# Chunk attention and token MLP: PSUM as two separate two-bank tiles used in turn, one evacuation per two output tiles and two transposed blocks, a new order of units

## The chip, the cores and the metric

The kernel runs on one core of one Trainium2 chip. Times are device microseconds (us) of one execution; each is the median of the runs named. Of 11 runs of the kernel before (176.16 to 180.61 us), 9 lie within a per cent of their median, 177.84 us. Runs more than 1.5% above the fastest of the same kernel in a call are set apart as slow, and ratios use the fast runs alone. A ratio is the mean time of one kernel's fast runs over that of the other's fast runs of the same rounds, so it is not quite the ratio of the medians that are quoted. The span of a profile is about 2 us shorter than the time of the same run. Experiments ran on three different chips, so versions of different calls are compared through their ratio to the kernel before of the same call.

Engines: PE is TensorE, DVE is VectorE, ACT is ScalarE, POOL is GpSimd.

## The reference, cut to what matters

```python
# q, k, v: (8, 8, 576, 64); chunks of 64 tokens attend only to themselves
scores = scale * q_c @ k_c.T;  attn = softmax(scores);  x = attn @ v_c      # x: (8, 576, 512)
# token MLP on x of each batch
wq = x @ w_q;  wk = x @ w_k                       # 512 -> 64
mixed = (wq @ wk.T * scale) @ x                   # (wq @ (wk.T @ x)) is cheaper
out = relu(mixed) @ w_out                         # 512 -> 512, float32
```

## The kernel before

One batch after the other goes through the same units, and each unit is a burst of matmuls on PE into PSUM and one evacuation by ACT or DVE. S is scores and exp (four per batch), A is attention times V with normalisation (four), X transposes one 128-wide block of x (four), Q and K are the two projections, G is wk.T @ x, M is one of four mixes with Relu, and O is one output tile of 128 rows (4.5 per batch). In iteration b the attention of batch b is interleaved with the MLP of batch b-1. PSUM is divided into four two-bank tiles: `st` for scores, `xp` for attention, `mp` for X, Q, G and M, and `op` for K and O.

```python
    mp = ps.tile([P, 2, 512], F32, name="mp")
    op = ps.tile([P, 2, 512], F32, name="op")
...
    def xtr(b, i, bank):
        tx = mp[:, bank, :].bitcast(F16)
        for j in range(NJ):
            nc.tensor.transpose(
                tx[:, j * P : j * P + P], xn[b % 2][:, j, i * P : i * P + P], ident[:]
            )
        nc.vector.tensor_copy(xt[b % 2][i][:], tx[:, 0 : NJ * P])
...
    def mix(b, i, half):
        for h in range(2):
            nc.tensor.matmul(
                mp[:, h, 0:HS],
                lhsT=g16[b % 2][CH * h : CH * h + CH, i * P : i * P + P],
                rhs=wqT[b % 2][CH * h : CH * h + CH, half * HS : half * HS + HS],
                ...
            )
        nc.scalar.activation(rmx..., mp[:, :, 0:HS], AF.Relu, scale=scale_moe)
...
    def o_(cnt=1):
            ...
            for i in range(NI):
                nc.tensor.matmul(
                    op[:, n % 2, :],
                    lhsT=rmx[pr % 2][:, i, tl * P : tl * P + P],
                    rhs=wout[:, i, :],
                    ...
                )
            nc.scalar.copy(os_[:], op[:, n % 2, :])
            nc.sync.dma_start(of[n * P : n * P + P, :], os_[:])
...
    # per batch:  S0 A3' X2' O S1 A0 X3' O Q' K' S2 A1 G' O S3 A2 M' M' O M' M' X0 O X1   (' = batch b-1)
```

The softmax here doesn't subtract the row's maximum and nothing guards it: scores larger than these inputs give would overflow.

## Time and profile before

| | before |
|---|---|
| median of 3 runs | 177.56 us (176.45 to 180.11) |
| profiled span (a run of 179.53 us, not one of the three) | 177.6 us |
| PE / DVE / ACT busy | 117.6 / 74.3 / 70.0 us |
| mean granted PE clock | 0.866 |
| last packet of the loads | 102 us |

These are lines of the first two parts of the page of the kernel before: busy time of PE in us and share of the span, then, over 40 equal slices of the span (4.4 us each), the granted PE clock and the busy share of the DMA engines in tenths.

```profile
PE 117.6 (66%) x2400; PEld 71.8 (40%) x2400; DVE 74.3 (42%) x149; ACT 70.0 (39%) x117; POOL 49.5 (28%) x49
...
PEclk9999999996599569987998899789969996996555
DMA  2999999999999999999999931113103111320322
```

No compute engine is full: the busiest, PE, is at 66%. The DMA engines are at 9 tenths or more in every slice but the first until about 102 us. The clock dips in each batch and stays low at the end: the clock record of the trace has PE at 0.5 in seven stretches of 3.4 or 6.8 us between 41.4 and 150.7 us, and from 160.9 us to the end.

This is the chain of waits of the kernel before, in order of time (start us, us, engine, tile, line). The steps shown are the second kT transpose of four successive batches.

```profile
82.65 0.66 DVE kT L118
...
100.73 0.66 DVE kT L118
...
117.85 0.66 DVE kT L118
...
134.49 0.66 DVE kT L118
```

The pattern repeats every 17.3 us on average. So a batch takes about 17 us although PE is busy for only 13.7 us of it.

These are groups of instructions of the kernel before: line, engine, operation, tiles, shape and count, then busy us in total and mean ns of one, then the idle time of the engine just before them and what ended it.

```profile
L254 PE MATMUL op<-wout,rmx 128*128 128x512 f16 x144 | 47.5, 462 | 3.1 <-ACT osb L262 3.1
L181 PE MATMUL mp<-ident,xn 128*128 128x128 f16 x160 | 19.1, 268 | 9.8 <-ACT rmx L236 5.2 <-DVE xt L184 4.3
L184 DVE COPY xt<-mp 128x640 f16<-128x640 f16 x32 | 15.5, 485 | 34.6 <-PE mp L181 34.6
L228 PE MATMUL mp<-wqT,g 64*128 64x288 f16 x64 | 10.4, 307 | 18.1 <-ACT rmx L236 17.2 <-issue 0.9
```

The mixes (L228) hold PE idle for 18.1 us, nearly all of it waiting for the Relu that reads the same tile. The timeline of the kernel before shows one such stretch (start us, us, engine, line, operation; in brackets the idle time before and its releaser):

```profile
126.11 0.30 PE L228 MATMUL mp<-wqT,g 64*128 64x288 f16 x2
126.53 0.66 ACT L236 ACTIVATE rmx<-mp 128x576 f16<-128x576 f32 x1
127.24 0.30 PE L228 MATMUL mp<-wqT,g 64*128 64x288 f16 x2 [0.83 <-ACT rmx L236]
127.57 0.65 ACT L236 ACTIVATE rmx<-mp 128x576 f16<-128x576 f32 x1 [0.39 <-PE mp L228]
128.28 0.30 PE L228 MATMUL mp<-wqT,g 64*128 64x288 f16 x2 [0.74 <-ACT rmx L236]
...
130.35 0.69 PE L181 MATMUL mp<-ident,xn 128*128 128x128 f16 x5 [0.74 <-ACT rmx L236]
```

PE works 0.30 us and waits 0.74 us, again and again: PE, ACT and PE go through one tile in single file. The transposes that follow take 0.69 us for five, against 0.45 elsewhere in the steady part; the clock record has PE at half its clock from 130.2 to 133.6 us (granted clock 0.50 there, 1.00 from 126.0 to 130.2).

One more place in the same timeline matters, the output tiles at the end. They alternate between the two banks of one tile, yet each waits for the copy out of the other bank:

```profile
163.58 0.59 ACT L262 COPY osb<-op 128x512 f32<-128x512 f32 x1 [1.22 <-PE op L254]
164.21 1.86 PE L254 MATMUL op<-wout,rmx 128*128 128x512 f16 x4 [0.72 <-ACT osb L262]
...
166.79 1.86 PE L254 MATMUL op<-wout,rmx 128*128 128x512 f16 x4 [0.72 <-ACT osb L262]
```

The copy at 163.58 ends at 164.17 and the matmuls of the other bank start at 164.21. In this program a wait covers the whole PSUM tile, not the bank. Two banks of one tile are therefore no double buffer here.

### The profile page before, as it was taken

How to read it: one execution, taken by the hardware profiler on the slowest of the kernel's cores; microseconds unless marked ns; L12 is line 12 of the kernel's file. 1: busy time of each engine (PE TensorE's matmuls, PEld its weight loads, DVE VectorE, ACT ScalarE, POOL GpSimd, SP SyncE). 2: the span in 40 equal slices, each digit the busy share in tenths (PEclk: the TensorE clock that was granted, in tenths of full speed). 3: DMA queues.
4: the chain of work that ended last, by engine and by line, in shares of the span. 5: the costliest groups of instructions: out<-in, count | busy, mean ns of one | idle time of the engine just before them, and what ended most of it. 6: DMA issues, size and time to landing. Idle time of an engine off the chain costs nothing.

```text
span 177.6 us, 5290 instructions
## 1 busy us (share of the span) xinstructions
PE 117.6 (66%) x2400; PEld 71.8 (40%) x2400; DVE 74.3 (42%) x149; ACT 70.0 (39%) x117; POOL 49.5 (28%) x49
## 2 busy tenths in 40 slices
PE   0024350693998499759964988589578957955861
PEld 0023240471665257426632564257236624622220
DVE  2332634534565365536461656275619422410000
ACT  2021111055246435654473437454634572344121
POOL 7997736647263273372000000000000000000000
PEclk9999999996599569987998899789969996996555
DMA  2999999999999999999999931113103111320322
GB/s 25 173 165 184 176 167 182 162 182 167 176 207 224 209 175 197 243 201 196 224 222 196 151 125 63 59 63 122 59 0 122 60 65 59 118 99 19 118 98 79
DMA packets 81156, 24.56 MB, mean 138 GB/s; under 512 B 76016, under 2 KB 76528, under 8 KB 81136
## 3 DMA queue, kind: packets, MB, share of 16 engines
q0 software_dynamic: 75952, 14.81, 98.5%
q1 hardware_dynamic: 5184, 9.44, 14.6%
q8 instruction: 18, 0.29, 0.7%
q14 instruction: 2, 0.02, 0.0%
HBM read 29.62 MB, written 9.44 MB: 220 GB/s over the span
## 4 chain that ended last, share of the span: by engine, by line
PE 44%; DVE 17%; ACT 17%; DMA 14%; issue 4%; POOL 2%; ACTq 0%; POOLq 0%
PE op L254 19%; ACT rmx L236 10%; DMA kn<-in_k_dram 8%; DVE xn L169 7%; DMA vt<-in_v_dram 6%; PE mp L189 6%; PE mp L181 5%; ACT osb L262 5%; PE mp L228 4%; DVE xt L184 4%; PE xp L159 3%; PE mp L217 3%; PE op L203 3%; DVE kT L118 3%; DVE qT L118 2%
## 5 line engine op out<-in xcount | busy, mean ns | idle before, releaser
L254 PE MATMUL op<-wout,rmx 128*128 128x512 f16 x144 | 47.5, 462 | 3.1 <-ACT osb L262 3.1
L262 ACT COPY osb<-op 128x512 f32<-128x512 f32 x36 | 21.1, 586 | 48.1 <-PE op L254 42.5
L142 ACT ACTIVATE est<-st 128x640 f16<-128x640 f32 (+1 forms) x32 | 20.9, 652 | 29.1 <-PE st L134 28.9
L184 DVE COPY xt<-mp 128x640 f16<-128x640 f16 x32 | 15.5, 485 | 34.6 <-PE mp L181 34.6
L169 DVE TENSOR_TENSOR xn<-xp,rec 128x640 f16<-128x640 f32 x32 | 26.4, 824 | 1.1
L181 PE MATMUL mp<-ident,xn 128*128 128x128 f16 x160 | 19.1, 268 | 9.8 <-ACT rmx L236 5.2
L236 ACT ACTIVATE rmx<-mp 128x576 f16<-128x576 f32 x32 | 20.9, 653 | 10.0 <-PE mp L228 9.9
L134 PE MATMUL st<-qT,kT 32*64 32x64 f16 x1152 | 17.9, 209 | 9.5 <-DVE kT L118 8.6
L254 PEld LDWEIGHTS <-rmx 128*128 128x128 f16 x144 | 14.4, 112 | 20.6 <-issue 14.5
L228 PE MATMUL mp<-wqT,g 64*128 64x288 f16 x64 | 10.4, 307 | 18.1 <-ACT rmx L236 17.2
L67 POOL DMA_DIRECT2D qn<-in_q_dram x16 | 16.1, 1005 | 18.8 <-DMA vt<-in_v_dram 16.7
L159 PE MATMUL xp<-vt,est 64*64 64x65 f16 x576 | 12.8, 211 | 12.6 <-DVE xn L169 7.5
L134 PEld LDWEIGHTS <-kT 32*64 32x64 f16 x1152 | 14.0, 121 | 17.1 <-DVE kT L118 8.6
L181 PEld LDWEIGHTS <-xn 128*128 128x128 f16 x160 | 14.4, 120 | 16.0 <-issue 14.2
L67 POOL DMA_DIRECT2D kn<-in_k_dram x16 | 16.0, 1001 | 8.8 <-DMA qn<-in_q_dram 4.5
L118 DVE STREAM_TRANSPOSE qT<-qn 128x576 f32<-128x576 f32 x16 | 12.4, 772 | 9.3 <-DMA qn<-in_q_dram 9.3
L73 POOL DMA_DIRECT2D vt<-in_v_dram x8 | 14.7, 1834 | 4.3 <-DMA kn<-in_k_dram 4.0
L159 PEld LDWEIGHTS <-est 64*64 64x64 f16 x576 | 10.0, 119 | 14.0 <-issue 12.2
L118 DVE STREAM_TRANSPOSE kT<-kn 128x576 f32<-128x576 f32 x16 | 12.0, 748 | 3.3 <-DMA kn<-in_k_dram 3.3
L228 PEld LDWEIGHTS <-g 64*128 64x128 f16 x64 | 3.2, 94 | 24.7 <-issue 24.0
L168 DVE RECIPROCAL rec<-xp 128x10 f32<-128x10 f32 x32 | 6.8, 213 | 15.3 <-PE xp L159 15.0
L189 PE MATMUL mp<-xt,wqd 128*128 128x288 f16 x64 | 10.1, 305 | 2.4 <-DVE xt L184 1.3
(22 smaller groups left out, 46.9 us busy)
## 6 DMA issues: line engine op xcount, KB each, us to landing
out_dram<-osb SPq DMA_DIRECT2D x36, 256.0 KB, 2.1
qn<-in_q_dram POOLq DMA_DIRECT2D x16, 288.0 KB, 16.6
kn<-in_k_dram POOLq DMA_DIRECT2D x16, 288.0 KB, 16.9
vt<-in_v_dram POOLq DMA_DIRECT2D x8, 576.0 KB, 18.7
wout<-in_moe_w_out_dram POOLq DMA_DIRECT2D x1, 512.0 KB, 9.4
wqd<-in_moe_w_q_dram POOLq DMA_DIRECT2D x1, 64.0 KB, 8.0
wk<-in_moe_w_k_dram POOLq DMA_DIRECT2D x1, 64.0 KB, 7.6
```

The source lines that it names most:

```text
L67: nc.gpsimd.dma_start(dst[b][part][:], src[b].rearrange("(t p r) d -> p t (r d)", p=P, r=R)[:, a:e, :],)
L118: nc.vector.transpose(out=o.rearrange("p (t w r) -> p t r w", r=R, w=32), in_=src[b][part].bitcast(F32).rearrange("p t (r d) -> p t r d", ...
L134: nc.tensor.matmul(st[half : half + CH, i // 2, (t - a) * CH : (t - a) * CH + CH], lhsT=operand(kT, b, t, i, e), rhs=operand(qT, b, t, i, ...
L142: nc.scalar.activation(est[b % 2][s].rearrange("p i t c -> p i (t c)")[:, :, 0:n], st[:, :, 0:n], AF.Exp, scale=scale_attn,)
L159: nc.tensor.matmul(xp[CH * (c % 2) : CH * (c % 2) + CH, hh, jj * 66 : jj * 66 + 65], lhsT=est[b % 2][s][half : half + CH, i // 2, t - SETS ...
L169: nc.vector.tensor_tensor(out=xn[b % 2][:, :, 2 * kk * D : 2 * kk * D + 2 * D].rearrange("p j (i d) -> p i j d", i=2), in0=xpv[:, :, :, 0: ...
L181: nc.tensor.transpose(tx[:, j * P : j * P + P], xn[b % 2][:, j, i * P : i * P + P], ident[:])
L184: nc.vector.tensor_copy(xt[b % 2][i][:], tx[:, 0 : NJ * P])
L189: nc.tensor.matmul(mp[:, h, 0:HS], lhsT=wqd[:, i, :], rhs=xt[b % 2][i][:, h * HS : h * HS + HS], start=(i == 0), stop=(i == NI - 1),)
L236: nc.scalar.activation(rmx[(b // 2) % 2].rearrange("p (h i) n -> p i h n", h=2)[:, i, :, o : o + HS], mp[:, :, 0:HS], AF.Relu, scale=scale ...
L254: nc.tensor.matmul(op[:, n % 2, :], lhsT=rmx[pr % 2][:, i, tl * P : tl * P + P], rhs=wout[:, i, :], start=(i == 0), stop=(i == NI - 1),)
L262: nc.scalar.copy(os_[:], op[:, n % 2, :])
```

## The change

The intent is that the two PSUM tiles of the MLP become a true double buffer. Every unit outside S and A takes the other tile than the unit before it (`pair()`). X handles two blocks at once with one DVE copy of 1280 columns in place of two of 640, and O handles up to two output tiles with one ACT copy of 1024 columns and one DMA. The units come in a new order that spreads the O and the DVE work.

```diff
+ORDER = """
+S0 A3 O2 X1 S1 A0 Tq0 Q K S2 A1 G O2 X0 S3 A2 Tk0 M0 M1 Tq1 O1 M2 M3 Tk1
+"""
...
-    mp = ps.tile([P, 2, 512], F32, name="mp")
-    op = ps.tile([P, 2, 512], F32, name="op")
+    rp = [ps.tile([P, 2, 512], F32, name=f"rp{i}") for i in range(2)]
...
+    def pair():
+        ring["at"] += 1
+        return rp[ring["at"] % 2]
+
+    def xtr(b, n):
+        tx = pair().bitcast(F16)
+        for i in range(2):
+            for j in range(NJ):
+                nc.tensor.transpose(
+                    tx[:, i, j * P : j * P + P],
+                    xn[b % 2][:, j, (2 * n + i) * P : (2 * n + i) * P + P],
+                    ident[:],
+                )
+        nc.vector.tensor_copy(xt[b % 2][n][:], tx[:, :, 0 : NJ * P])
...
+    def mix(b, n):
+        i, half = n % 2, n // 2
+        a = pair()
...
+    def outp(most):
...
+        a = pair()
+        for u in range(m):
...
+        nc.scalar.copy(os_[:, 0:m, :], a[:, 0:m, :])
+        nc.sync.dma_start(
+            of[n * P : (n + m) * P, :].rearrange("(u p) m -> p u m", p=P),
+            os_[:, 0:m, :],
+        )
```

In the order, Tq and Tk are the stream transposes of q and k of the next batch on DVE; A3, X1, Q, K, G, M and O belong to batch b-1.

More of the change, by code (lines that the diff above doesn't have):

```diff
@@ L99 @@
     xn = [sb.tile([P, NJ, DM], F16, name=f"xn{i}") for i in range(2)]
-    xt = [[sb.tile([P, NJ * P], F16, name=f"xt{i}_{c}") for c in range(NI)] for i in range(2)]
+    xt = [[sb.tile([P, 2, NJ * P], F16, name=f"xt{i}_{c}") for c in range(2)] for i in range(2)]
     wqT = [sb.tile([P, S], F16, name=f"wqT{i}") for i in range(2)]
@@ L104 @@
     rmx = [sb.tile([P, NI, 2 * S], F16, name=f"rmx{i}") for i in range(2)]
-    NOSB = 6
-    osb = [sb.tile([P, DM], F32, name=f"osb{i}") for i in range(NOSB)]
+    NOSB = 4
+    osb = [sb.tile([P, 2, DM], F32, name=f"osb{i}") for i in range(NOSB)]
     for i in range(B):
@@ L112, with tr @@
         nc.vector.memset(xv[i][CH:P, NJ - 1, D : D + 2], 1.0)
-    def tr(b, part):
+    def tr(b, which):
+        part = int(which[1])
         a, e = TR[part]
-        for src, dst in ((qn, qT), (kn, kT)):
-            o = dst[b % 2].bitcast(F32)[:, CH * a : CH * e]
-            nc.vector.transpose(
-                out=o.rearrange("p (t w r) -> p t r w", r=R, w=32),
-                in_=src[b][part].bitcast(F32).rearrange("p t (r d) -> p t r d", d=32),
-            )
+        src, dst = (qn, qT) if which[0] == "q" else (kn, kT)
+        nc.vector.transpose(
+            out=dst[b % 2]
+            .bitcast(F32)[:, CH * a : CH * e]
+            .rearrange("p (t w r) -> p t r w", r=R, w=32),
+            in_=src[b][part].bitcast(F32).rearrange("p t (r d) -> p t r d", d=32),
+        )
     def operand(buf, b, t, i, e):
@@ L176, in attend, with mlp_q @@
         )
-    def xtr(b, i, bank):
-        tx = mp[:, bank, :].bitcast(F16)
-        for j in range(NJ):
-            nc.tensor.transpose(
-                tx[:, j * P : j * P + P], xn[b % 2][:, j, i * P : i * P + P], ident[:]
-            )
-        nc.vector.tensor_copy(xt[b % 2][i][:], tx[:, 0 : NJ * P])
-    def wq_(b):
+    ring = {"at": 0}
+    def pair():
[11 more added lines that the diff above has]
+        nc.vector.tensor_copy(xt[b % 2][n][:], tx[:, :, 0 : NJ * P])
+    def mlp_q(b):
+        a = pair()
         for i in range(NI):
@@ L189, in wq_ @@
                 nc.tensor.matmul(
-                    mp[:, h, 0:HS],
+                    a[:, h, 0:HS],
                     lhsT=wqd[:, i, :],
-                    rhs=xt[b % 2][i][:, h * HS : h * HS + HS],
+                    rhs=xt[b % 2][i // 2][:, i % 2, h * HS : h * HS + HS],
                     start=(i == 0),
@@ L196, in wq_, with mlp_k @@
         nc.scalar.copy(
-            wqT[b % 2].rearrange("p (h n) -> p h n", h=2), mp[:, :, 0:HS]
+            wqT[b % 2].rearrange("p (h n) -> p h n", h=2), a[:, :, 0:HS]
         )
-    def wk_(b, pool, bank):
+    def mlp_k(b):
+        a = pair()
         for j in range(NJ):
@@ L203, in wk_ @@
                 nc.tensor.matmul(
-                    pool[:, bank, j * DH : j * DH + DH],
-                    lhsT=xt[b % 2][i][:, j * P : j * P + P],
+                    a[:, 0, j * DH : j * DH + DH],
+                    lhsT=xt[b % 2][i // 2][:, i % 2, j * P : j * P + P],
                     rhs=wk[:, i, :],
@@ L210, in wk_, with mlp_g @@
         nc.vector.tensor_copy(
-            wkn[b % 2].rearrange("p j c -> p (j c)"), pool[:, bank, 0 : NJ * DH]
+            wkn[b % 2].rearrange("p j c -> p (j c)"), a[:, 0, 0 : NJ * DH]
         )
-    def gm_(b, bank):
+    def mlp_g(b):
+        a = pair()
         for j in range(NJ):
@@ L217, in gm_ @@
                 nc.tensor.matmul(
-                    mp[CH * h : CH * h + CH, bank, 0 : DM // 2],
+                    a[CH * h : CH * h + CH, 0, 0 : DM // 2],
                     lhsT=wkn[b % 2][:, j, :],
@@ L223, in gm_ @@
                 )
-        nc.scalar.copy(g16[b % 2][:], mp[:, bank, 0 : DM // 2])
-    def mix(b, i, half):
+        nc.scalar.copy(g16[b % 2][:], a[:, 0, 0 : DM // 2])
+    of = out.rearrange("b s m -> (b s) m")
+    done = {"out": 0, "ready": 0, "st": 0}
+    def mix(b, n):
+        i, half = n % 2, n // 2
+        a = pair()
         for h in range(2):
             nc.tensor.matmul(
-                mp[:, h, 0:HS],
+                a[:, h, 0:HS],
                 lhsT=g16[b % 2][CH * h : CH * h + CH, i * P : i * P + P],
@@ L237, in mix @@
             rmx[(b // 2) % 2].rearrange("p (h i) n -> p i h n", h=2)[:, i, :, o : o + HS],
-            mp[:, :, 0:HS],
+            a[:, :, 0:HS],
             AF.Relu,
@@ L241, in mix @@
         )
-    of = out.rearrange("b s m -> (b s) m")
-    state = {"n": 0, "ready": 0}
-    def o_(cnt=1):
-        for _ in range(cnt):
-            n = state["n"]
-            if n >= state["ready"]:
-                return
-            state["n"] = n + 1
-            pr, tl = n // NCH, n % NCH
+        if i == 1:
+            done["ready"] = ((2 * b + half + 1) * HS) // P
+    def outp(most):
+        n = done["out"]
+        m = min(most, done["ready"] - n, NCH - n % NCH)
+        if m <= 0:
+            return
+        done["out"] = n + m
+        a = pair()
+        for u in range(m):
+            pr, tl = (n + u) // NCH, (n + u) % NCH
             for i in range(NI):
                 nc.tensor.matmul(
-                    op[:, n % 2, :],
+                    a[:, u, :],
                     lhsT=rmx[pr % 2][:, i, tl * P : tl * P + P],
@@ L260, in o_ @@
                 )
-            os_ = osb[n % NOSB]
-            nc.scalar.copy(os_[:], op[:, n % 2, :])
-            nc.sync.dma_start(of[n * P : n * P + P, :], os_[:])
-    tr(0, 0)
-    tr(0, 1)
+        os_ = osb[done["st"] % NOSB]
+        done["st"] += 1
+        nc.scalar.copy(os_[:, 0:m, :], a[:, 0:m, :])
+        nc.sync.dma_start(
+            of[n * P : (n + m) * P, :].rearrange("(u p) m -> p u m", p=P),
+            os_[:, 0:m, :],
+        )
+    for w in ("q0", "k0", "q1", "k1"):
+        tr(0, w)
@@ L267 @@
     for b in range(B + 1):
         p = b - 1
-        if b < B:
-            scores(b, 0)
-        if p >= 0:
-            attend(p, 3)
-            xtr(p, 2, 0)
-        o_()
-        if b < B:
-            scores(b, 1)
-            attend(b, 0)
-        if p >= 0:
-            xtr(p, 3, 1)
-            o_()
-            if p == 0:
-                nc.vector.tensor_copy(wqd[:, :, DH : 2 * DH], wqd[:, :, 0:DH])
-            wq_(p)
-            wk_(p, op, state["n"] % 2)
-            state["n2"] = 1
@@ L286 @@
-        if b < B:
-            scores(b, 2)
-            attend(b, 1)
-        if p >= 0:
-            gm_(p, 0)
-            o_()
-        if b < B:
-            scores(b, 3)
-            attend(b, 2)
-        if b + 1 < B:
-            tr(b + 1, 0)
-        if p >= 0:
-            for half in range(2):
-                for i in range(2):
-                    mix(p, i, half)
-                    if i == 1 and half == 0:
-                        o_()
-            state["ready"] = (NCH * b) // 2
@@ L304 @@
-        if b < B:
-            xtr(b, 0, 0)
-            o_()
-            xtr(b, 1, 1)
-        if b + 1 < B:
-            tr(b + 1, 1)
-    o_(10)
+        for w in ORDER.split():
+            if w[0] == "T":
+                if b + 1 < B:
+                    tr(b + 1, w[1:])
+            elif w[0] == "O":
+                outp(int(w[1]))
+            elif w[0] == "S":
+                if b < B:
+                    scores(b, int(w[1]))
+            elif w[0] == "A":
+                kk = int(w[1])
+                bb = p if kk == 3 else b
+                if 0 <= bb < B:
+                    attend(bb, kk)
+            elif w[0] == "X":
+                i = int(w[1])
+                bb = p if i else b
+                if 0 <= bb < B:
+                    xtr(bb, i)
+            elif p >= 0:
+                if w == "Q":
+                    if p == 0:
+                        nc.vector.tensor_copy(wqd[:, :, DH : 2 * DH], wqd[:, :, 0:DH])
+                    mlp_q(p)
+                elif w == "K":
+                    mlp_k(p)
+                elif w == "G":
+                    mlp_g(p)
+                elif w[0] == "M":
+                    mix(p, int(w[1]))
@@ L314 @@
+    while done["out"] < done["ready"]:
+        outp(2)
 _INS = ['q', 'k', 'v', 'moe_w_q', 'moe_w_k', 'moe_w_out']
```

## The prediction

> **What bounds the kernel now.** By the page PE is 66% busy, DVE 42, ACT 39. Input DMA is at 9 tenths until about 100 us (slices), but from 47 us nothing waits for it. The chain of waits shows a repeating period: the same kT transpose starts at 65.3, 82.7, 100.0, 117.2 and 134.5 us, 17.3 us a batch. In the stretch 99.55 to 116.67 PE is busy 13.7, DVE 9.0 and ACT 8.7 of 17.1 us; start to start, at the fast clock, I add up the PE units to about 11.6 us. So 5 to 6 us of each period are waits and slow-clock matmuls: PSUM hand-overs:
>
> - The four mixes share one tile: each waits for the Relu read of the previous (list of waits: mix for ACT 17.2 us in 21 waits; first transpose after them 5.2). A mix takes 0.30 us, a Relu 0.65, so a mix costs about 1.04 us, and mixes to first transpose take 4 to 4.7 us per batch.
> - Waits go by whole tile, not by bank: in the last five output tiles the matmuls (other bank) start 0.05 us after the copy of the tile before ended, at 164.21, 166.79, 169.38, 171.96.
> - After the mixes PE is slow: the next output tile takes 1.91 us against 1.03 for the same four matmuls elsewhere, transposes 0.69 against 0.45; about 1.2 us a batch. [...]
>
> **What the change does.** Two really separate tiles alternate over all twelve units, so each unit waits for the unit before last.
> Evacuations: ACT copies of 256, 512, 640 columns take 372, 586, 704 ns, so 1024 should take about 1.01 us instead of 2 x 0.586; output copies fall from 36 to 24, saving about 2 us of ACT in total. DVE transposed copies 640 at 0.485; 1280 estimated 0.82, saving 0.15 us each, 2.4 in total. Both mostly lie off the critical path; the gain must come from the hand-overs.
>
> **Walk of one new period** with these durations and 0.05 us hand-over: mixes with the output unit between them about 3.0 us; scores, last attend, two outputs and transposes to 6.6; scores, attend and the wait for the 0.82 us copy to 7.6; Q, K, to 9.2; scores, attend, G to 10.7; two outputs, transposes to 13.5; scores, attend to 14.2. With five output tiles 14.3, with four 13.4; with clock losses 14 to 14.5. DVE (9.3) and ACT (8.6) fit.
>
> Start: unchanged up to the first normalisation after the batch-1 load (30.6 us); batch 2 is then held near 44 (before 48.5) partly by loads, about 12 us a batch. Six periods of about 14.2 bring the last batch's attend to about 129 (before 150.3). Tail: before 27.2 us; now copies overlap matmuls; I count 24, partly at half clock. Sum: 153.5 us.
>
> Predicted 153.5 us, range 148 to 160; faster by over 2%: 0.97, same 0.02, slower 0.01.
>
> **What would show it.** Right: period 14 to 14.6 between successive kT transposes; mix waits on ACT under a third of 17.2 us; output copies about 1.01 us, transposed copies about 0.82; output matmuls near 1.03 us per four in the steady part; last attend to end about 24 us.
> Wrong if: the strict alternation makes PE wait on a DVE copy queued behind stream transposes (period over 15); PE stays at half clock; loads slow down or become the limit (DVE waits for qn, kn after 45 us); the two-tile output DMA lengthens the end by more than 1 us.

One sentence of the recorded text is cut where it is marked. The traces show a granted clock of 0.90 from 99.55 to 116.67 us and of 0.69 from 150.44 us to the end. 153.5 us is about 129 us to the last attend and about 24 us of tail.

## More of the kernel before

All loads of q, k and v are issued by GpSimd in one stream from the start, with a cast from float32 to float16 on the way, each batch into its own tiles. No compute unit holds a load back.

## The result, and the profile after

| | before | after |
|---|---|---|
| median (4 runs each) | 178.09 us | 155.75 us (154.79 to 157.33) |
| ratio of fast runs | | 0.8754, 95% interval 0.8654 to 0.8855 |
| profiled span | 177.6 us | 152.8 us |
| PE busy | 117.6 us | 105.9 us |
| mean granted PE clock | 0.866 | 0.952 |
| half-clock stretches, in sum | 49.6 us | 17.0 us |

The half-clock stretches are the sum of the stretches that the clock record of the trace lists at 0.5; the last one runs some 2 us past the end of the span.

These lines of the page of the changed kernel answer to those shown of before (busy us, clock and DMA in 40 slices of 3.8 us):

```profile
PE 105.9 (69%) x2400; PEld 66.0 (43%) x2400; DVE 72.3 (47%) x133; ACT 66.0 (43%) x105; POOL 49.5 (32%) x49
...
PEclk9999999999999985799999985799999999999998
DMA  1999999999999999999999999994131130323325
```

The regular dips of the clock are gone, but two long ones have come, from 56.1 to 62.9 and from 90.2 to 97.0 us by the clock record, both while the loads still run. These are the groups of the changed kernel:

```profile
L277 PE MATMUL rp<-wout,rmx 128*128 128x512 f16 x144 | 40.3, 413 | 4.7 <-ACT rmx L258 4.7
L193 PE MATMUL rp<-ident,xn 128*128 128x128 f16 x160 | 13.6, 235 | 8.2 <-DVE xn L174 8.1
L198 DVE COPY xt<-rp 128x1280 f16<-128x1280 f16 x16 | 13.2, 825 | 25.0 <-PE rp L193 21.3 <-ACT osb L286 3.6
L286 ACT COPY osb<-rp 128x1024 f32<-128x1024 f32 x12 | 12.1, 1012 | 19.3 <-PE rp L277 12.5 <-issue 6.8
L250 PE MATMUL rp<-wqT,g 64*128 64x288 f16 x64 | 9.7, 305 | 4.5 <-ACT osb L286 4.1
```

The idle time before the mixes fell from 18.1 to 4.5 us. The output matmuls and the transposes, the same work, take 12.7 us less PE time (47.5 + 19.1 before, 40.3 + 13.6 after). The timeline of the changed kernel shows the mixes of one batch:

```profile
116.49 0.69 PE L250 MATMUL rp<-wqT,g 64*128 64x288 f16 x4
116.83 1.19 ACT L258 ACTIVATE rmx<-rp 128x576 f16<-128x576 f32 x2
117.53 0.39 PE L277 MATMUL rp<-wout,rmx 128*128 128x512 f16 x1 [0.35 <-ACT rmx L258]
118.08 0.82 PE L277 MATMUL rp<-wout,rmx 128*128 128x512 f16 x3 [0.15 <-ACT rmx L258]
118.83 0.30 PE L250 MATMUL rp<-wqT,g 64*128 64x288 f16 x2
119.61 0.30 PE L250 MATMUL rp<-wqT,g 64*128 64x288 f16 x2 [0.49 <-ACT osb L286]
```

Four mixes and an output tile take 3.4 us from 116.49 to the next scores at 119.84; before, four mixes alone took 4.2 us up to the transposes. The last output tiles no longer wait for each other's copies; the last four of them stand in one line:

```profile
144.36 3.61 PE L277 MATMUL rp<-wout,rmx 128*128 128x512 f16 x16 [0.25 <-ACT rmx L258]
```

The same timeline shows something that the prediction had not looked for. PE stops in the middle of a unit, between two matmuls with nothing to wait for that the profile shows, and after the longest stop falls to half the clock (the output matmuls at 92.80 take 3.60 us for eight, against 1.90 elsewhere):

```profile
84.86 0.31 PE L164 MATMUL xp<-vt,est 64*64 64x65 f16 x13
87.90 0.25 PE L164 MATMUL xp<-vt,est 64*64 64x65 f16 x5 [2.73 <-issue]
...
92.80 3.60 PE L277 MATMUL rp<-wout,rmx 128*128 128x512 f16 x8
```

The list of waits gives these stops to "issue", which means that the profile shows nothing that PE waited for (engine, tile, line, releaser, then us in total, times, longest us):

```profile
PE xp L164 <- issue: 3.4, 2, 2.7
...
PE st L139 <- issue: 1.0, 1, 1.0
PE rp L219 <- issue: 1.0, 1, 1.0
```

The second kT transposes of the changed kernel start at 44.00, 57.55, 74.23, 90.53, 106.66 and 119.08 us. The periods are 13.6, 16.7, 16.3, 16.1 and 12.4 us, so three batches that run beside the loads take about 4 us more than the one after them (its neighbours with one output tile more would take 13.3 us, as a later run shows).

To see what the stops are, PE's instructions (weight loads and matmuls) were counted in the trace. The changed kernel has 4800, and PE stops exactly before numbers 1471, 1983, 2495 and 2751, each 191 more than a multiple of 256. The DMA records hold 19 packets of 16384 bytes on the instruction queue, one for about every 256 PE instructions. A few of them, taken from the trace records of the changed kernel (the second column assumes that a packet is asked for when PE passes the previous such boundary; a stop is counted from the start of the PE instruction before it, so it is about 0.2 us longer than the idle time in the list above):

```
packet  PE passes previous boundary   packet starts   packet ends   PE passes next boundary
   4              48.30                   52.02           52.96        54.46  after a stop of 1.2
   6              63.54                   65.22           66.20        67.68  after a stop of 0.9
   8              75.19                   79.02           79.97        81.43  after a stop of 1.1
   9              81.43                   85.64           86.54        87.90  after a stop of 2.9
  (loads end at 103.9)
  14             113.18                  114.09          115.17       120.03  no stop
  15             120.03                  121.37          122.33       125.08  no stop
```

At each stop PE goes on 1.4 to 1.5 us after the packet ended. While the loads run ten of the twelve packets start 3.3 to 4.4 us after the boundary, the other two 1.1 and 1.7 us after it. Once the loads have ended five of seven start 0.7 to 1.3 us after it, and two (0.4 and 1.5 us) before it, so the assumption about when a packet is asked for does not hold for those. That these packets bring PE's instructions, and that PE waits for them at the stops, is inferred from the name of the queue, from their number and from these times. The estimate from these numbers: a block of 256 instructions whose packet starts about 4 us after the boundary takes at least about 4 + 0.95 + 1.45 = 6.4 us, and at that pace the 600 PE instructions of a batch take about 15 us. Not every packet is late: packet 6 started after 1.7 us, and its block took 4.1 us.

### The profile page after: what moved, and what is told of

It is laid out like the page before. It is cut to its first block, busy times and chain, and to the rows that moved or that the text cites. A ratio compares the mean times of both kernels' runs of the same rounds, so it can differ in the third digit from the quotient of the medians.

```text
span 152.8 us, 5231 instructions
## 1 busy us (share of the span) xinstructions
PE 105.9 (69%) x2400; PEld 66.0 (43%) x2400; DVE 72.3 (47%) x133; ACT 66.0 (43%) x105; POOL 49.5 (32%) x49
## 5 line engine op out<-in xcount | busy, mean ns | idle before, releaser
L277 PE MATMUL rp<-wout,rmx 128*128 128x512 f16 x144 | 40.3, 413 | 4.7 <-ACT rmx L258 4.7
L286 ACT COPY osb<-rp 128x512 f32<-128x512 f32 (+1 forms) x24 | 19.2, 799 | 30.2 <-PE rp L277 17.5
L139 PE MATMUL st<-qT,kT 32*64 32x64 f16 x1152 | 17.5, 207 | 12.4 <-DVE kT L121 10.5
L198 DVE COPY xt<-rp 128x1280 f16<-128x1280 f16 x16 | 13.2, 825 | 25.0 <-PE rp L193 21.3
L277 PEld LDWEIGHTS <-rmx 128*128 128x128 f16 x144 | 13.0, 103 | 23.5 <-ACT rmx L258 8.8
L71 POOL DMA_DIRECT2D qn<-in_q_dram x16 | 16.1, 1006 | 19.2 <-DMA vt<-in_v_dram 16.2
L139 PEld LDWEIGHTS <-kT 32*64 32x64 f16 x1152 | 13.7, 119 | 15.9 <-DVE kT L121 10.7
L258 ACT ACTIVATE rmx<-rp 128x576 f16<-128x576 f32 x32 | 19.3, 653 | 2.8 <-PE rp L250 2.8
L193 PE MATMUL rp<-ident,xn 128*128 128x128 f16 x160 | 13.6, 235 | 8.2 <-DVE xn L174 8.1
L71 POOL DMA_DIRECT2D kn<-in_k_dram x16 | 16.1, 1003 | 9.2 <-DMA kn<-in_k_dram 5.9
L193 PEld LDWEIGHTS <-xn 128*128 128x128 f16 x160 | 11.2, 106 | 12.7 <-DVE xn L174 8.9
L250 PE MATMUL rp<-wqT,g 64*128 64x288 f16 x64 | 9.7, 305 | 4.5 <-ACT osb L286 4.1
L204 PE MATMUL rp<-xt,wqd 128*128 128x288 f16 x64 | 10.2, 307 | 2.6 <-DVE wqd L318 2.0
L211 ACT CAST wqT<-rp 128x576 f16<-128x576 f32 x8 | 5.1, 638 | 9.5 <-PE rp L204 9.5
## 6 DMA issues: line engine op xcount, KB each, us to landing
qn<-in_q_dram POOLq DMA_DIRECT2D x16, 288.0 KB, 16.7
```

The source lines that it names most:

```text
L71: nc.gpsimd.dma_start(dst[b][part][:], src[b].rearrange("(t p r) d -> p t (r d)", p=P, r=R)[:, a:e, :],)
L139: nc.tensor.matmul(st[half : half + CH, i // 2, (t - a) * CH : (t - a) * CH + CH], lhsT=operand(kT, b, t, i, e), rhs=operand(qT, b, t, i, ...
L193: nc.tensor.transpose(tx[:, i, j * P : j * P + P], xn[b % 2][:, j, (2 * n + i) * P : (2 * n + i) * P + P], ident[:],)
L198: nc.vector.tensor_copy(xt[b % 2][n][:], tx[:, :, 0 : NJ * P])
L258: nc.scalar.activation(rmx[(b // 2) % 2].rearrange("p (h i) n -> p i h n", h=2)[:, i, :, o : o + HS], a[:, :, 0:HS], AF.Relu, scale=scale_moe,
L277: nc.tensor.matmul(a[:, u, :], lhsT=rmx[pr % 2][:, i, tl * P : tl * P + P], rhs=wout[:, i, :], start=(i == 0), stop=(i == NI - 1),)
```

## The experiments

Theory A: the gain comes from the alternation of two tiles. Theory B: it comes from the new order and the pairing. Theory C: it comes from fewer evacuations. The first four runs go through combinations of the three parts.

### The old order with tiles in turn

```diff
-    mp = ps.tile([P, 2, 512], F32, name="mp")
-    op = ps.tile([P, 2, 512], F32, name="op")
+    rp = [ps.tile([P, 2, 512], F32, name=f"rp{i}") for i in range(2)]
+    def pair(): ...                       # as in the change
     def xtr(b, i, bank):
-        tx = mp[:, bank, :].bitcast(F16)
+        tx = pair()[:, bank, :].bitcast(F16)
# wq_, gm_, mix:  mp = pair();  each output tile:  op = pair();  wk_(p, pair(), 0)
```

> The kernel before in its old order and with single evacuations, but its two PSUM tiles used in turn by every unit. Theory A (the alternation of two tiles carries the gain): about 161 us, waits of mixes for ACT fall from 17.2 us to about 8. Theory B (the new order and the paired units carry it): 170 us or more.

Measured: 154.88 us median, ratio to before 0.8766 (interval 0.870 to 0.883). That is the whole gain of the change, more than expected, with none of its other parts. The list of waits of this run, the mixes:

```profile
PE rp L236 <- ACT rmx L244: 3.9, 9, 0.7
PE rp L236 <- issue: 2.2, 1, 2.2
PE rp L236 <- ACT osb L271: 1.9, 4, 0.5
```

The mixes wait 5.8 us for ACT in place of 17.2. Theory A holds.

### The new order with tiles fixed by kind

```diff
-    def pair():
-        ring["at"] += 1
-        return rp[ring["at"] % 2]
+    def pair(which=0):
+        return rp[which]                  # K and outputs: pair(1)
```

> The changed kernel with its new order and merged evacuations, but the tiles fixed by kind as before (one for transposes, Q, G and mixes, one for K and outputs). Theory A: about 170 us, mixes wait for ACT again about 14 us or more in total. Theory B: 160 us or less.

Measured: 178.98 us median of four runs that do not agree: one of 172.37 (the profiled one, the only one counted as fast) and three of 178.5 to 180.9. No ratio can be formed. In the profiled run the mixes wait 14.1 us for ACT. Even the best run has lost most of the gain, and theory B's 160 is excluded.

### The change with split evacuations

```diff
-        nc.vector.tensor_copy(xt[b % 2][n][:], tx[:, :, 0 : NJ * P])
+        for i in range(2):
+            nc.vector.tensor_copy(xt[b % 2][n][:, i, :], tx[:, i, 0 : NJ * P])
-        nc.scalar.copy(os_[:, 0:m, :], a[:, 0:m, :])
+        for u in range(m):
+            nc.scalar.copy(os_[:, u, :], a[:, u, :])
```

> The changed kernel with each merged evacuation split again into two copies out of the same two-bank tile; 12 more copies on ACT and 16 more on DVE, each with about 0.16 us of fixed cost. Theory A (copies lie off the critical path): 155.5 to 158 us. Rival C (fewer evacuations are what pays): 161 us or more.

Measured: 156.17 us, ratio 0.8856 (0.876 to 0.895). The changed kernel had 0.8754 in its first comparison and 0.8850 in a later one, so the merged copies are worth less than these runs can resolve. The fixed cost named agrees with the profiles of the kernels before and after, where two single copies take 0.16 us more than a merged one on ACT (2 x 0.586 - 1.012) and 0.145 us more on DVE (2 x 0.485 - 0.825). Theory C falls.

### Both undone, the new order alone

The edit is the sum of the last two.

> The new order alone: tiles fixed by kind and evacuations split. Theory A: 170 to 174 us, close to the kernel before. Theory B (order): 162 us or less.

Measured: 177.59 us median; the two fast runs are 174.87 and 175.62, ratio 0.9913 (0.979 to 1.004). This is no different from the kernel before, as theory A says; the fast runs lie 0.9 and 1.6 us above the range expected. The new order by itself gives nothing here that these runs can resolve.

So why does the new order with pairing add nothing to the alternation? The stops named a suspect: while the loads run, PE gets its instructions too slowly (theory D), and a better order cannot use what it saves.

### The change with few loads (wrong result)

```diff
-    qn = [[sb.tile(... name=f"qn{i}_{a}") for a, b in TR] for i in range(B)]
+    qn = [[sb.tile(... name=f"qn{i}_{a}") for a, b in TR] for i in range(2)] * (B // 2)   # kn, vt alike
-    for b in range(1, B):
+    for b in range(1, 2):
         load_qk(b, 0)
```

> The changed kernel, wrong result on purpose: only batches 0 and 1 are loaded, batches 2 to 7 compute on the same two sets of tiles. In the changed kernel PE stopped in the middle of units at instruction numbers 1471, 1983, 2495 and 2751, all 191 beyond a multiple of 256, while the loads ran, and a 16384-byte packet of the instruction queue ended 1.4 to 1.5 us before PE went on. Theory D (instruction fetches of PE queue behind the loads): no such stops after batch 1, fetch delay about 1 us in place of about 4, every period 12.4 or 13.3 us, 144 us. Rival E (the stops belong to PE and its units, not to the loads): 154 us or more.

Measured: 143.26 us, ratio 0.7981 (0.796 to 0.801). The profiled run is the slow one of the four (145.71 us). It has no stop before any of the boundaries after the first batch, the packets start at most 1.6 us after the boundary (the last packet, behind which no work waits, excepted), and the periods between second kT transposes are 12.5, 13.3, 12.4, 13.3 and 12.4 us. Even in this slow run half-clock stretches sum to 6.0 us. What theory D expected came about, and theory E falls: the loads cost the changed kernel 12 us by the medians (155.75 and 143.26, of two calls), or 14 us by the ratios (0.8754 - 0.7981 = 0.077 of 179.4). The two profiles show where. Up to PE instruction 1215 they lie within 0.6 us of each other (48.3 us with the loads, 48.8 without), so late data at the start is not the reason. From 1215 to 3263 the changed kernel takes 54.9 us and this run 43.7. Of these 11.2 us, 6.2 lie in the four blocks of 256 that end in a stop (23.0 against 16.8 us) and 5.1 in the two blocks without a stop that hold the two half-clock stretches of 6.8 us (18.8 against 13.7 us); the other two blocks are alike within 0.1 us. That the stops bring on the half clock is inferred from their order in time, and what in the loads delays a packet is not shown.

### The kernel before with few loads (wrong result)

The same edit on the kernel before.

> The kernel before, wrong result on purpose, with only batches 0 and 1 loaded. Theory D: before was slow enough that its fetches hardly showed (stops of about 2 us in all), so 174 to 178 us. If instead loads held before as much as after, 168 us or less.

Measured: 176.56 us, ratio 0.9809 (0.975 to 0.987). The loads cost the kernel before only about 3 us. Without loads the change would be worth 33 us (176.6 to 143.3); beside them it is worth 22.

### At most two loads under way

```diff
+    def turn(dst):
+        if len(landed) >= 2:
+            nc.gpsimd.tensor_copy(sink[:, 0:1], landed[-2])
+        landed.append(dst)
         for src, dst in ((qf, qn), (kf, kn)):
+            turn(dst[b][part][:, 0, 0:1])
             nc.gpsimd.dma_start(
```

> The changed kernel, right result, where GpSimd reads one column of the load before the last before it issues the next, so that at most two loads are under way. If the fetch delay comes from the number of loads queued: delay falls from about 4 to about 2 us, about 148 us. If a fetch shares the engines with whatever load is running: same delay, 155 to 158 us. If two loads cannot fill the engines: loads end later than 110 us and 160 us or more.

Measured: 183.46 us, ratio 1.0211 (1.017 to 1.025), result right. The last load packet ends at 150.5 us in place of 104, so the times of the third outcome came about, and the kernel waits for its data (DVE 28.7 us for kn and 27.2 us for qn in the page of this run). Its reason is not shown: that page has the DMA engines at 9 tenths in 29 of the 32 slices up to 147.5 us. In the profile (of the slowest of its four runs) packets of the instruction queue still started 2.7 to 5.2 us after the boundary in seven of 18 blocks, and sooner in others; in a kernel that waits for its data this does not tell whether the number of queued loads sets the delay. That stays open.

### The kernel before, kept warm

```diff
+    def warm(n):
+        for _ in range(n):
+            nc.tensor.matmul(st[:, 1, :], lhsT=ident[:], rhs=wout[:, 0, :], start=True, stop=True)
     def mix(b, i, half):
+        if (i, half) != (0, 0):
+            warm(2)
...
+            warm(2)                        # after the last mix
```

> The kernel before with two idle 128x512 matmuls into unread columns of the score tile before each waiting mix and after the last. The waits for the Relu stay; only PE is kept active in them. Theory F (half of the gain is clock, not waits): the output tile after the mixes takes 1.03 us instead of 1.91, granted clock above 0.93, about 168 us. Theory G (the clock is a symptom that costs little): 175 us or more.

Measured: 168.07 us, ratio 0.9372 (0.934 to 0.941), result right; the waits are filled with matmuls whose output nobody reads, and the granted clock is 0.988. The group of output matmuls in this run:

```profile
L262 PE MATMUL op<-wout,rmx 128*128 128x512 f16 x144 | 37.1, 380 | 3.1 <-ACT osb L270 3.1
```

They take 37.1 us in place of 47.5. The single-file hand-over is left as it was, as the timeline of this run shows: the mixes and the transposes after them still start 1.04 us apart (L228 is here the idle matmul), and only the five transposes are faster, 0.44 us in place of 0.69.

```profile
108.11 0.29 PE L236 MATMUL mp<-wqT,g 64*128 64x288 f16 x2
108.34 0.61 PE L228 MATMUL st<-wout,ident 128*128 128x512 f16 x2
109.15 0.30 PE L236 MATMUL mp<-wqT,g 64*128 64x288 f16 x2 [0.20 <-ACT rmx L244]
109.38 0.60 PE L228 MATMUL st<-wout,ident 128*128 128x512 f16 x2
110.19 0.44 PE L181 MATMUL mp<-ident,xn 128*128 128x128 f16 x5 [0.20 <-ACT rmx L244]
```

So the clock alone gives half of the gain: 1 - 0.9372 = 0.063 of 1 - 0.8766 = 0.123 for the alternation. Theory F holds. PE waits cost twice here, once as idle time and once as half clock in the work that follows.

### The old order with tiles in turn, and few loads (wrong result)

> Wrong result on purpose: the old order with the tiles in turn (the run that was as fast as the whole change), with only batches 0 and 1 loaded. The changed kernel with few loads took 143.3 us. Theory D (new order and pairing do save PE waits, but while the loads run the fetches of PE set the pace and hide it): 148 to 152 us here, so the new order is worth 3 to 6% where loads are away. If the new order is worth nothing in itself: 142 to 145 us.

Measured: 149.43 us, ratio 0.8414 (0.837 to 0.846), against 0.7981 for the change with few loads. So the new order and the merged units are worth about 5% where no loads run (0.7981 / 0.8414 = 0.949), and nothing beside them. The gain of the order is real, but it is lost beside the loads. The profiles agree with late packets of the instruction queue as the taker: from PE instruction 959 to 3263, nine blocks, the old order took 60.0 us and the new one 61.9 beside the loads, but 54.0 and 50.7 without them, and in the old order with tiles in turn every one of these nine packets started 3.9 to 4.5 us after the boundary.

### A version with repaired start and end

```diff
+FIRST = "S0 S1 A0 S2 A1 X0 S3 A2 Tq0 Tk0"
+SECOND = "S0 A3 X1 S1 A0 Q K Uq1 Uk1 S2 A1 G X0 S3 A2 Tq0 Tk0 M0 M1 Tq1 O1 M2 M3 Tk1"
+LAST = "A3 O2 X1 Q K G O2 M0 M1 M2 M3 O2 O2 O1"
...
+        if b == B - 1 and i == 1:
+            nc.vector.tensor_scalar(out=dst, in0=a[:, :, 0:HS], scalar1=scale_moe, scalar2=0.0,
+                                    op0=ALU.mult, op1=ALU.max)
...
+        if n >= B * S // P - 8:            # last outputs: one tile by ACT, one by DVE, a DMA for each
```

Uq1 and Uk1 are the stream transposes of the running batch.

> The changed kernel, right result, with two repairs that follow from the trace. Start: the stream transposes of batch 1 are queued behind the normalisations of batch 0 on DVE, so that the token MLP of batch 0 runs while PE would wait for loads; expected 3 to 5 us. End: in the last batch DVE takes half of the Relu and of the output copies, and each output tile leaves alone; expected 2 to 3 us. Together about 149 us. If fetches pace PE from the start, the early lead is lost again before the loads end and only the end is won: 152 to 153 us.

Measured: 153.80 us, ratio 0.8672 (0.862 to 0.872), result right. The unaltered change, on the same chip:

> The changed kernel unaltered, on the same chip as the two other runs of this call, for comparison: 155.5 us, within 1%.

Measured: 156.67 us, ratio 0.8850 (0.880 to 0.890). The repaired version is about 2% faster than the change (0.8672 / 0.8850) and the best measured. In the profiles it reaches PE instruction 959 at 37.8 us against 41.5, but instruction 3263, when the loads have just ended, at 102.3 against 104.5. So 3.7 us of lead shrank to 2.3 beside the loads, and the end added the rest. Neither time named beforehand came about (149 us, or 152 to 153 us if the lead is lost); the second is the nearer, but a part of the lead was kept.

### Outputs spread while the loads run

```diff
+SPREAD = "S0 A3 O1 X1 S1 O1 A0 Tq0 Q K S2 A1 G O1 S3 X0 A2 Tk0 M0 M1 Tq1 O1 M2 M3 O1 Tk1"   # iterations 2 to 5
```

> The version with repaired start and end (153.8 us), and in iterations 2 to 5, while the loads run, the output tiles one by one between the units of many small matmuls, so that PE uses its instructions up more evenly. Theory D: a block of 256 PE instructions takes no less than about 6.4 us while the loads run (delay 4, transfer 0.95, 1.45 until PE goes on); the changed kernel takes 7.2 us a block there, the old order with tiles in turn 6.7 us. Expected 6.7 to 6.8 us a block, no stop longer than 2 us, less half clock, 150 to 151.5 us. If the rate of fetches did not set the pace: 153 us or more.

The 6.4 us of this expectation are the estimate given with the packets above, not a measured bound.

Measured: 154.95 us median, but the six runs go from 152.23 to 156.43, and four of them count as slow, so no ratio can be formed. In its profile (152.2 us span) a block between instructions 1215 and 3007 takes 7.0 us, not 6.7 to 6.8; a stop of 3.7 us remains, and half-clock stretches sum to 18.4 us. The version that it alters took 7.3 us a block there, so the blocks did get shorter. This is a miss: spreading the outputs by hand did not give a dependable gain. By time alone it even falls on the side named for the rival (153 us or more if the rate of fetches did not set the pace). The eight packets of the blocks from 1215 to 3263 still started 2.6 to 4.3 us after the boundary, so this run does not count against late packets, but it does not confirm that an even use of instructions cures them.

## Why the prediction was right or wrong

The time was right: 155.75 us measured against 153.5 predicted, within 148 to 160. The main cause was right too, the single-file use of PSUM tiles and the slow clock that goes with it (granted clock 0.866 in the profile of the kernel before, 0.988 with its waits filled). The total is closer than its terms, since two errors cancel.

- "Waits go by whole tile, not by bank": right. Only the run with tiles in turn gets the gain; the same units with fixed tiles lose it.
- "A mix costs about 1.04 us", and mix waits fall under a third of 17.2 us: right. They fell to 4.1 us in the changed kernel.
- Slow clock "about 1.2 us a batch": right, and nearly in size. Keeping the kernel before warm gave a ratio of 0.937, about 11 us in all. By the two profiles 6.1 us of it lie in the six periods from 47.6 to 150.3 us (102.8 against 96.7 us, 1.0 us a batch) and 3.9 us in the tail (27.3 against 23.4 us), where the last output tiles take 1.86 us each and which the prediction counted apart.
- Evacuations estimated at 1.01 and 0.82 us: measured 1.012 and 0.825. For ACT three measured widths stood behind the estimate, for DVE one (640 columns at 0.485) and an assumed saving of 0.15 us, measured as 0.145. That they lie off the critical path was right as well, by the run with split copies.
- "Walk of one new period": the sum came out too long. Undisturbed periods are 12.4 us with four output tiles and 13.3 with five (the run with few loads), not 13.4 and 14.3. A mis-sized term is the transposes: the walk took 0.9 us for ten (2 x 0.45), and ten in a row take 0.72 us with the next unit starting after 0.65. The assumed wait of Q for the 0.82 us copy did not appear either.
- "With clock losses 14 to 14.5", as the period between kT transposes: this step failed. Its own sign of failure, a period over 15, came, though not by the DVE queue that it named: the periods are 16.1 to 16.7 us for three batches beside the loads and 12.4 after them. The walk had no term for the stops at late packets of the instruction queue; the mean over the six batches, 14.6 us from attend to attend (45.2 to 133.1 us), only happens to look like it. The prediction did list "loads slow down or become the limit" as a risk, but looked for it as DVE waiting for q and k, where it was not to be seen: from 45 to 104 us the list of waits has no compute engine that waits for a load.
- "Batch 2 is then held near 44": 45.2 us. "I count 24" us for the tail "partly at half clock": 19.7 us (133.1 to 152.8). The last 16 output matmuls ran at full clock, 3.61 us in all, which is a part of the difference; the rest is not worked out.
- "DVE (9.3) and ACT (8.6) fit": right, both stayed under 50% busy.
- A slip in the reading: of the five starts quoted for "the same kT transpose", 100.0 and 117.2 are those of the qT transpose just before; the kT ones are 100.73 and 117.85. The period of 17.3 us stands.

## What to carry to other kernels

Look at which unit of storage a wait covers: in this program it was the whole tile, so two banks of one tile went in single file (0.72 us of wait for each of the last output tiles), and giving consecutive units two separate tiles was worth 12% (ratio 0.8766), by itself the whole gain of a much larger rewrite. Idle gaps on PE cost twice here, since the matmuls after them ran at half clock (1.91 us for an output tile in place of 1.03); filling the gaps with idle matmuls brought the granted clock from 0.866 to 0.988 and showed cheaply how large that half is (6% of the time). When many small matmuls run beside loads that keep the DMA engines at 9 tenths, count PE's instructions. Here it stopped inside a unit, for 0.9 to 2.9 us, at four places that lie multiples of 256 instructions apart, each 1.4 to 1.5 us after the end of a packet of the instruction queue, hence the suspicion against the fetches. Neither a better order (0.8766 without it, 0.8754 with it) nor fewer evacuations (0.8856 without, 0.8850 with) gained anything measurable while those packets were late.
